# Downsampled and local attention with mixture of experts: value products in 64-row pieces, P^T in one copy, full transposes of q and k, values loaded 256 keys at a time

## The chip, the cores and the metric

The kernel runs on one core of a Trainium2 chip. The metric is the device time of one execution in microseconds (us), and lower is better. The engines are TensorE (PE, with its weight loads PEld), VectorE (DVE), ScalarE (ACT), GpSimd (POOL) and SyncE (SP, which here only issues transfers). SBUF is the working memory of 128 partitions, PSUM the memory of eight banks that PE writes.

## What is computed

There are 8 batches of 8 heads, 576 positions and 64 numbers per head. Two attentions are added, and the sum goes through eight experts, each of which takes a fixed number of tokens:

```
q_d, k_d, v_d = means of q, k, v over 4 neighbouring positions
out_up    = repeat(softmax(q_d k_d^T / 8) v_d, 4)
out_local = softmax(where(|i-j| < 4, q k^T / 8, -1e9)) v
x = (out_up + out_local) as 4608 rows of 512
logits = x w_gate;  tokens are assigned greedily, 576 to each expert
out[tokens of e] = relu(x w1[e]) w2[e]
```

## The kernel before

The program has two stages. The class `Attention` makes x and the gate's logits, and then `Routing` and `Experts` pick the tokens of one expert after another and run its two products. The change touches the attention stage alone.

**Local attention** goes by tiles: a tile u is four windows of 32 queries, so there are 36 tiles and 4.5 tiles to a batch. A window sees 38 keys. One tile passes through these steps, each of them a piece of work for PE:

- `loc_s` (line 430): 32 products of 64 rows by 32 columns, scores of 32 queries against 38 keys, into a PSUM tile "s" of two banks. DVE takes the maxima and subtracts (lines 439 and 440), and ACT exponentiates (line 442) into `sw`.
- `loc_t` (line 450): four transposes of 128x128 into a tile "g" of one bank. ACT copies it out in two copies of 64 partitions (line 461), into `ptw`, in which the blocks of two windows stand beside zeros, so that one product of 128 rows can serve two windows.
- `loc_v` (line 472): 16 products of 128 rows by 64 columns with the values `vw`, in two halves of one "g" bank each. `norm` (lines 397, 398 and 400) divides each half on DVE.
- `log_a`, `store`, `log_t` and `log_m`: DVE adds the upsampled part `up` (line 480), SP stores x, PE transposes x (line 490) and forms the logits.

**Per batch**, `trw` (line 292) turns q and k so that the 64 numbers of a head lie on partitions: eight times per batch, each time eight products of a 64-column piece with the identity, into one "g" bank that one copy of 128 partitions empties (`evac`, line 278 on ACT or line 276 on DVE). `trt` does the same for the last 64 positions. `gsum` sums groups of four on POOL and DVE, and `down_s`, `down_t` and `down_v` are the downsampled attention.

**The order** is written by hand. `run` gives each piece a due time in tiles (`LOC` for the tile's steps, `TW` and `TWS` for the transposes, `DW` for the downsampled part, `NEXT` for the loads of the next batch), sorts all pieces by it and emits them. Every engine then works through its own list in that order, and so does SP with its transfers. "g" has six buffers (`NG`) and "s" one, which is all eight banks. A transfer on SP also waits for the transfer eight places ahead of it.

**Values for the local part** are loaded by tile: `load_vw` (line 228) issues four transfers per tile, each 48 keys of one window for all eight heads, into one of four buffers. `EV` says which of the copies in `evac` go to DVE (1) and which to ACT (0), once the first 24 are past.

## Time and profile before

| what | value |
|---|---|
| median of 3 runs | 780.48 us (778.41 to 783.68) |
| profiled execution | 776.94 us, span 775.3 us (1.6 us lie around it) |
| PE busy over the span | 710.1 us (92%) |
| DVE, ACT, POOL busy | 526.9, 306.2, 222.4 us |
| attention stage | until about 288 us |

The span is the time from the first to the last instruction of the profile. "Busy" counts the time in which at least one instruction of the engine runs. Matmuls overlap in the array, so the time that a group of them costs is better read from the start of the group to the start of the next one. In a timeline row stand the start, the length, the engine, the line, what is written from what, and the count. fp32 products appear twice in the count, as two passes.

### The profile page before, as it was taken

How to read it: one execution, taken by the hardware profiler on the slowest of the kernel's cores; microseconds unless marked ns; L12 is line 12 of the kernel's file. 1: busy time of each engine (PE TensorE's matmuls, PEld its weight loads, DVE VectorE, ACT ScalarE, POOL GpSimd, SP SyncE). 2: the span in 40 equal slices, each digit the busy share in tenths (PEclk: the TensorE clock that was granted, in tenths of full speed). 3: DMA queues.
4: the chain of work that ended last, by engine and by line, in shares of the span. 5: the costliest groups of instructions: out<-in, count | busy, mean ns of one | idle time of the engine just before them, and what ended most of it. 6: DMA issues, size and time to landing. Idle time of an engine off the chain costs nothing.

```text
span 775.3 us, 22696 instructions
## 1 busy us (share of the span) xinstructions
PE 710.1 (92%) x9393; PEld 493.1 (64%) x9393; DVE 526.9 (68%) x1634; ACT 306.2 (39%) x601; POOL 222.4 (29%) x257
## 2 busy tenths in 40 slices
PE   7998999899999863699899999999989999999994
PEld 5887888787878752465465466465456475574752
DVE  3876785858667887886969989798859545271210
ACT  2444645456464440341624435144225144252210
POOL 6345262424426340300710503130320402201011
PEclk9999999999999995699999999999999999999998
DMA  9969979898998650611615554572833764704000
GB/s 262 220 191 245 241 209 262 227 242 246 235 234 200 163 176 3 209 70 62 244 36 208 144 171 157 106 268 56 258 117 110 156 245 95 199 1 102 21 28 34
DMA packets 148138, 125.09 MB, mean 161 GB/s; under 512 B 92228, under 2 KB 122436, under 8 KB 148036
## 3 DMA queue, kind: packets, MB, share of 16 engines
q1 hardware_dynamic: 140656, 102.12, 48.6%
q0 software_dynamic: 6432, 20.98, 8.9%
q8 instruction: 74, 1.21, 0.7%
q10 hardware_dynamic: 948, 0.55, 0.3%
q14 instruction: 28, 0.23, 0.1%
HBM read 95.30 MB, written 21.23 MB: 150 GB/s over the span
## 4 chain that ended last, share of the span: by engine, by line
PE 44%; issue 25%; DVE 18%; POOL 4%; DMA 4%; ACT 2%; another core or an unknown queue 1%; SPq 0%; POOLq 0%; ACTq 0%; DVEq 0%
PE g L292 8%; PE pH L1109 8%; PE pX L1148 6%; PE g L472 3%; POOL out_dram L1157 2%; DVE cmp L698 2%; PE g L318 2%; PE s L430 2%; DVE wl L1055 2%; PE g L366 2%; PE g L450 2%; PE pR L728 2%; PE g L490 1%; PE g L363 1%; DVE ht L1135 1%
## 5 line engine op out<-in xcount | busy, mean ns | idle before, releaser
L1109 PE MATMUL pH<-xt,wh 128*128 128x256 f16 (+1 forms) x1024 | 200.0, 289 | 1.7 <-ACT xt L1084 0.7
L1148 PE MATMUL pX<-wh,ht 128*128 128x512 f16 (+1 forms) x640 | 180.6, 380 | 1.9 <-DVE xt L1085 1.9
L1109 PE MATMUL pH<-xt,wl 128*128 128x320 f16 (+1 forms) x512 | 147.7, 289 | 0.0
L1148 PEld LDWEIGHTS <-ht 128*128 128x128 f16 (+1 forms) x960 | 81.6, 100 | 90.4 <-issue 5.9
L1157 POOL DMA_INDIRECT out_dram<-y,idx x40 | 44.9, 1123 | 282.5 <-ACT y L1154 260.2
L1148 PE MATMUL pX<-wl,ht 128*128 128x512 f16 (+1 forms) x320 | 117.9, 380 | 0.0
L1109 PEld LDWEIGHTS <-wh 128*128 128x128 f16 x1024 | 97.9, 98 | 28.3 <-issue 3.4
L1132 ACT ACTIVATE ht<-pH 128x512 f16<-128x512 f32 (+1 forms) x128 | 45.5, 408 | 126.4 <-PE pH L1109 123.9
L1055 DVE SCALAR_TENSOR_TENSOR wl<-nat,wh 128x512 f16<-128x512 f32 x128 | 84.8, 684 | 2.2
L1070 POOL DMA_INDIRECT xg<-x_dram,idx x40 | 49.2, 1231 | 103.9 <-DVE idx L999 34.5
L1135 DVE SCALAR_TENSOR_TENSOR ht<-pH,ht 128x512 f16<-128x512 f32 (+1 forms) x128 | 52.6, 451 | 33.8 <-ACT ht L1132 33.3
L1154 ACT ACTIVATE y<-pX 128x512 f32<-128x512 f32 (+1 forms) x40 | 23.7, 594 | 129.7 <-PE pX L1148 76.4
L292 PE MATMUL g<-ident,nat 128*64 128x128 f32 x1024 | 69.8, 282 | 0.7 <-issue 0.3
L1053 ACT ACTIVATE wh<-nat 128x1024 f16<-128x1024 f32 x64 | 66.6, 1056 | 9.3 <-DMA nat<-in_moe_w_dram 9.2
L292 PEld LDWEIGHTS g<-ident,nat 128*64 128x64 f32 x1024 | 56.4, 139 | 8.0 <-issue 3.7
L1109 PEld LDWEIGHTS <-wl 128*128 128x128 f16 x512 | 50.4, 98 | 12.4 <-issue 0.4
L461 ACT COPY pt<-g 64x512 f32<-64x512 f32 x72 | 41.7, 579 | 25.3 <-PE g L450 24.5
L1156 DVE SCALAR_TENSOR_TENSOR y<-pX,y 64x512 f32<-64x512 f32 x8 | 5.5, 693 | 59.1 <-ACT y L1154 59.0
L472 PE MATMUL g<-vw,pt 128*64 128x65 f32 x1152 | 43.4, 226 | 1.9 <-DMA x_dram<-x 0.9
L472 PEld LDWEIGHTS g<-vw,pt 128*64 128x64 f32 x1152 | 38.1, 139 | 7.7 <-ACT pt L461 3.9
L278 ACT COPY qt<-g 128x512 f32<-128x512 f32 (+1 forms) x32 | 19.0, 593 | 43.6 <-PE g L292 37.0
L728 PEld LDWEIGHTS <-cmp 128*128 128x128 bf16 x504 | 20.2, 97 | 24.2 <-DVE cmp L698 12.3
(218 smaller groups left out, 1137.2 us busy)
## 6 DMA issues: line engine op xcount, KB each, us to landing
nat<-in_moe_w_dram SPq DMA_DIRECT2D x28, 1024.0 KB
vw<-in_v_dram SPq DMA_DIRECT2D x136, 96.0 KB
up<-up_dram SPq DMA_DIRECT2D x36, 256.0 KB
x_dram<-x SPq DMA_DIRECT2D x36, 256.0 KB
nat<-in_q_dram SPq DMA_DIRECT2D x16, 512.0 KB
nat<-in_k_dram SPq DMA_DIRECT2D x16, 512.0 KB
nat<-in_v_dram SPq DMA_DIRECT2D x14, 512.0 KB
up_dram<-xu SPq DMA_DIRECT2D x16, 128.0 KB
```

What stands on the lines that cost most here:

```text
L292: nc.tensor.matmul(p[64 * s:64 * s + 64, :, f], src[:, 2 * hp + s, f], self.ident, start=True, stop=True)
L461: self.nc.scalar.copy(out, in_)
L472: nc.tensor.matmul(o[64 * i:64 * i + 64, 65 * h:65 * h + 65], pt[:, 2 * (h % 2) + i, 2 * g + h // 2].rearrange("p b q -> p (b q)"), self.v ...
L728: mm = nc.tensor.matmul(cv[:m * J, :, :m], cmp[:, t:t + m].rearrange("p t j -> p (t j)"), oh[:, :, t:t + m], start=t == 0, stop=t + m == N ...
L1053: nc.scalar.activation(hi, r, AF.Copy, scale=sc)
L1055: nc.vector.scalar_tensor_tensor(lo[:, a:a + LOP], r[:, a:a + LOP], sc, hi[:, a:a + LOP], op0=OP.mult, op1=OP.subtract)
L1070: self.fetched = nc.gpsimd.indirect_dma_start(out=xg[:n], out_offset=None, in_=self.x, in_offset=bass.IndirectOffsetOnAxis(ap=idx[:n, c:c ...
L1109: mm = nc.tensor.matmul(p[:, s, :s1 - s0], w[d][a][:, 128 * f:128 * f + 128], xt[:, b, d, s0:s1], start=j == 0, stop=j == len(seq) - 1)
L1132: last = nc.scalar.activation(hi, q, AF.Relu)
L1135: nc.vector.scalar_tensor_tensor(lo, q, 0.0, hi, op0=OP.max, op1=OP.subtract)
L1148: mm = nc.tensor.matmul(p[o:o + m], ht[:, f, h0:h0 + m], w[4 + f // 2][b][:, 512 * (f % 2):512 * (f % 2) + 512], start=j < parts, stop=j > ...
L1157: i = nc.gpsimd.indirect_dma_start(out=self.out, in_=y[:n], in_offset=None, out_offset=bass.IndirectOffsetOnAxis(ap=idx[:n, c:c + 1], axis=0))
```

## The change

It does five things.

1. `trw` uses full transposes of 128x128: two of the four positions of a group and their 64 numbers at once. There are four of them per call, for two pairs of heads and one half of each pair. The result stands on two halves of the partitions, so two copies of 64 partitions empty the bank, both on the same engine.
2. `loc_t` empties its bank in one copy of 128 partitions by 512 (`ptw` loses its zeros), and `sw` is ordered by window first.
3. `loc_v` makes a product for each window and head, 64 rows by 32 columns, at positions in the array that depend on the head's half and the window. It writes to a tile "s" of two banks, and one division serves the whole tile of 128x512.
4. The pool "g" has four buffers and "s" two.
5. Values are loaded by head in groups of eight windows (`load_vw`), eight transfers per group and two groups per batch; the first and last window of a batch are loaded apart (`load_ve`). There are three buffers of a group. Of `evac`'s calls one in four goes to DVE.

```diff
-NG = 6
+NG = 4
+NS = 2
-EV = (0,)
+EV = (0,0,0,1)
+VG = 8
+VS = 0.06
...
+    def load_ve(self, b, w):
...
+            for i in range(2):
+                p0 = 64 * i + r0
+                nc.sync.dma_start(self.ve[b % 2][p0:p0 + n, int(w > 0), :, :D],
...
+    def load_vw(self, b, w, m, h):
+        n, i = divmod(w - 1, VG)
+        t = self.vw[(2 * b + n) % 3]
+        p0 = 64 * (h % 2)
+        self.nc.sync.dma_start(t[p0:p0 + VR, i:i + m, h // 2, :D],
...
-        for f in range(4):
-            for s in range(2):
-                nc.tensor.matmul(p[64 * s:64 * s + 64, :, f], src[:, 2 * hp + s, f], self.ident, start=True, stop=True)
-        self.evac(self.dest(b, which)[:, hp, :4 * GM], p.rearrange("p g f -> p (g f)"))
+        for a in range(2):
+            for fp in range(2):
+                nc.tensor.transpose(p[:, a, :, fp], src[:, 4 * hh + 2 * a + s, 2 * fp:2 * fp + 2].rearrange("p f d -> p (f d)"),
+                                    self.ident)
+        t = self.dest(b, which)[64 * s:64 * s + 64, 2 * hh:2 * hh + 2]
+        for par in range(2):
+            self.evac(t[:, :, par:4 * GM:2], p[64 * par:64 * par + 64].rearrange("p a i f -> p a (i f)"), par)
...
-            self.pevac(a, out[r, :, :, a], p[r].rearrange("p (i h q) -> p i h q", h=4, q=QW))
+        nc.scalar.copy(self.ptw[u % NPT].rearrange("p c h q -> p (c h q)"), p)
...
-        for h in range(4):
-            for i in range(2):
-                nc.tensor.matmul(o[64 * i:64 * i + 64, 65 * h:65 * h + 65],
-                                 pt[:, 2 * (h % 2) + i, 2 * g + h // 2].rearrange("p b q -> p (b q)"),
-                                 self.vw[u % 4][:, i, 4 * g + h], start=True, stop=True)
-        self.norm(o, x[:, 256 * g:256 * g + 256].rearrange("p (h d) -> p h d", h=4), 4, 1.0)
+        for hp in range(HP):
+            for c, vw in cs:
+                for i in range(2):
+                    r = slice(64 * i, 64 * i + 64)
+                    nc.tensor.matmul(o[32 * c:32 * c + 32, i, hp], pt[r, c, hp], vw[r, hp], start=True, stop=True,
+                                     tile_position=(64 * i, 32 * c))
+        if g == 0:
+            return
...
+        nc.vector.tensor_scalar(r, o[..., D], 1e-9, None, op0=OP.add)
+        nc.vector.reciprocal(r, r)
+        nc.vector.tensor_tensor(x.rearrange("p (h i d) -> p i h d", i=2, d=D), o[..., :D],
+                                r[..., None].to_broadcast([128, 2, HP, D]), op=OP.mult)
```

The order of the pieces stays the same; what stands in them changes. On PE, behind the third batch's `trt`, before (natt, sd and nat are the sources of the transposes, vw and pt those of the value products):

```order
L302 MATMUL g<-ident,natt 64x128 x8
L348 MATMUL g<-ident,sd 128x128 x3
L472 MATMUL g<-vw_128,pt_132 64x65 x16
L348 MATMUL g<-ident,sd 128x128 x3
L292 MATMUL g<-ident,nat 64x128 x8
L348 MATMUL g<-ident,sd 128x128 x3
L353 MATMUL g<-ident,sdt 128x128 x2
L292 MATMUL g<-ident,nat 64x128 x8
L450 MATMUL g<-ident,sw_129 128x128 x4
```

And now:

```order
L316 MATMUL g<-ident,natt 64x128 x8
L362 MATMUL g<-ident,sd 128x128 x3
L479 MATMUL s<-vw_126,pt_133 32x65 x32
L362 MATMUL g<-ident,sd 128x128 x3
L303 MATMUL g<-ident,nat 128x128 x4
L362 MATMUL g<-ident,sd 128x128 x3
L367 MATMUL g<-ident,sdt 128x128 x2
L303 MATMUL g<-ident,nat 128x128 x4
L464 MATMUL g<-ident,sw_130 128x128 x4
```

No row moved. Eight products of 64 columns became four of 128, and sixteen value products became thirty-two, which write to "s" instead of "g".

On ACT, in the same batch, the copies out of the banks before (qt and kt are the turned q and k, ptd and pt the transposed probabilities):

```order
L278 COPY ptd<-g 128x384
L278 COPY qt<-g 128x512
L278 COPY ptd<-g 128x384
L278 COPY ptd<-g 128x256
L278 COPY kt<-g 128x512
L461 COPY pt_132<-g 64x16x32 x2
L278 COPY qt<-g 128x512
L442 ACTIVATE sw_129<-sw_129 128x8x38
```

And now:

```order
L289 COPY ptd<-g 128x384
L289 COPY qt<-g 64x2x256 x2
L289 COPY ptd<-g 128x384
L289 COPY kt<-g 64x2x256 x2
L466 COPY pt_133<-g 128x512
L289 COPY qt<-g 64x2x256 x2
L456 ACTIVATE sw_130<-sw_130 128x8x38
```

Each copy of q or k became two, the two copies of pt became one, and one of the ptd copies went to DVE.

On SP, around the end of a batch's downsampled part (up_dram and up carry it through memory), before:

```order
L380 DMA up_dram<-xu 128x256
L387 DMA up_dram<-xu 8x16x64
L409 DMA up<-up_dram 128x1x512
L228 DMA vw_126<-in_v_dram 48x8x64 x3
L228 DMA vw_126<-in_v_dram 32x8x64
L228 DMA vw_126<-in_v_dram 6x8x64
L214 DMA nat<-in_q_dram 128x4x256
L483 DMA x_dram<-x 128x512
L214 DMA nat<-in_k_dram 128x4x256
L409 DMA up<-up_dram 128x1x512
L214 DMA nat<-in_v_dram 128x4x256
L228 DMA vw_127<-in_v_dram 48x8x64 x4
```

And now:

```order
L394 DMA up_dram<-xu 128x256
L401 DMA up_dram<-xu 8x16x64
L423 DMA up<-up_dram 128x1x512
L232 DMA ve_129<-in_v_dram 32x4x64 x2
L232 DMA ve_129<-in_v_dram 6x4x64 x2
L215 DMA nat<-in_q_dram 128x4x256
L497 DMA x_dram<-x 128x512
L215 DMA nat<-in_k_dram 128x4x256
L423 DMA up<-up_dram 128x1x512
L215 DMA nat<-in_v_dram 128x4x256
L232 DMA ve_128<-in_v_dram 48x4x64 x2
L240 DMA vw_127<-in_v_dram 48x8x64 x5
```

The other transfers stand where they stood. The value loads come in runs of eight now, and a batch has 22 of them where it had 19.

More of the change, by code (lines that the diff above doesn't have):

```diff
@@ L126, in __init__ @@
             self.vd.append(cst.tile([128, 2, H, D + 1], F32, name=f"vd{i}"))
-        for i in range(4):
-            self.vw.append(cst.tile([128, 2, H, D + 1], F32, name=f"vw{i}"))
+        for i in range(3):
+            self.vw.append(cst.tile([128, VG, HP, D + 1], F32, name=f"vw{i}"))
+        for i in range(2):
+            self.ve.append(cst.tile([128, 2, HP, D + 1], F32, name=f"ve{i}"))
         for i in range(NSW):
@@ L131, in __init__ @@
         for i in range(NPT):
-            self.ptw.append(cst.tile([128, 4, 4, 2, QW], F32, name=f"pt{i}"))
+            self.ptw.append(cst.tile([128, 4, HP, QW], F32, name=f"pt{i}"))
     def gate(self):
@@ L148, in fixed @@
         if part == 0:
-            for t in self.vw[:2]:
+            for t in (self.ve[0], self.vw[0]):
                 nc.gpsimd.memset(t, 1.0)
@@ L418, in loc_s @@
         if g == 0:
-            self.so[u] = self.ps.tile([128, 2, 512], F32, name="s", bufs=1)
+            self.so[u] = self.ps.tile([128, 2, 512], F32, name="s", bufs=NS)
             for i in range(2):
@@ L451, in loc_t @@
                                 self.ident)
-        out = self.ptw[u % NPT]
-        for a in range(2):
-            r = slice(64 * a, 64 * a + 64)
-            self.pevac(a, out[r, :, :, a], p[r].rearrange("p (i h q) -> p i h q", h=4, q=QW))
-    def pevac(self, a, out, in_):
-        if PEV[a]:
-            self.nc.vector.tensor_copy(out, in_)
-        else:
-            self.nc.scalar.copy(out, in_)
+        nc.scalar.copy(self.ptw[u % NPT].rearrange("p c h q -> p (c h q)"), p)
     def loc_v(self, u, g):
@@ L514, in transposes, with f @@
         out = []
-        for hp in range(HP):
-            for w in "qk":
-                def f(w=w, hp=hp):
-                    self.trw(b, w, hp)
-                    if b and hp % 2 and w == "k":
-                        self.gsum(b, "k", hp - 1)
-                        self.gsum(b, "q", hp - 1)
-                        if hp == 3:
-                            self.gsum_v(b)
-                out.append(f)
+        for hh in range(2):
+            for s in range(2):
+                for w in "qk":
+                    def f(w=w, hh=hh, s=s):
+                        self.trw(b, w, hh, s)
+                        if b and s and w == "k":
+                            self.gsum(b, "k", 2 * hh)
+                            self.gsum(b, "q", 2 * hh)
+                            if hh:
+                                self.gsum_v(b)
+                    out.append(f)
         return out[:2] + [lambda: self.trt(b)] + out[2:]
@@ L597, in run @@
                     work += [(at + SPACE * k, 3, k, lambda g=steps: next(g, None), False) for k in range(24)]
+        for b in range(B):
+            for w in (0, NW - 1):
+                if b or w:
+                    work.append(((b * NW + w) // 4 - VWT, 0, 0, lambda b=b, w=w: self.load_ve(b, w), False))
+            for n in range(2):
+                z = b * NW + 1 + VG * n
+                at = z // 4 - VWT
+                old = z - (NW + 1 if n else 2 * NW + 1 - 2 * VG)
+                if old > 0:
+                    at = max(at, old // 4 + LOC["v1"] + 0.0005)
+                for w, m, at in ((1, 3, LD0[2] + 0.01), (4, 5, LD0[3])) if at < -1.0 else ((1 + VG * n, VG, at),):
+                    for h in range(H):
+                        work.append((at + VS * h, 0, h, lambda b=b, w=w, m=m, h=h: self.load_vw(b, w, m, h), False))
         work.sort(key=lambda z: z[:3])
```

52 lines of the change are left out of this document (26 added, 26 removed).

## The prediction

> **What bounds the kernel now.** The change lies in the attention stage, so I first read busy time by stretch. The columns are the stretch, its length, then the busy time of PE, PEld, DVE, ACT and POOL, the granted clock of PE, the busy share of the DMA engines and their GB/s.
>
> ```profile
> 20.00:260.00 240.00, 229.38 (x5186) 193.68 (x5185) 174.71 (x483) 127.19 (x268) 103.08 (x138) 0.99 0.91 229
> ```
>
> PE is busy in 229.4 of 240 us; 10.6 us are idle. No other engine comes near: DVE 73%, ACT 53%. The transfers are at 0.91. The chain of waits through the same stretch says which work sets the pace:
>
> ```profile
> by line: PE g L292 22.5%; PE g L472 10.2%; PE g L318 6.6%; PE s L430 5.5%; PE g L450 5.4%; PE g L366 4.9%; PE g L490 4.1%; PE g L348 4.0%; PE g L363 3.6%; issue 2.8%; PE g L302 2.6%; DVE gtmp L265 2.5%; ACT pt L461 1.9%; DVE x L480 1.9%; PE
> ```
>
> The transposes of q and k (L292) are 22.5% of it and the value products (L472) 10.2%, and both are rewritten. So PE sets the pace, and what the change does to PE's work is nearly the whole gain or loss, until the next resource is reached. That one is SP with its transfers:
>
> ```profile
> 129.39 2.22 SPq L228 DMA_DIRECT2D vw<-in_v_dram  x4
> 132.19 0.35 SPq L483 DMA_DIRECT2D x_dram<-x  x1
> 132.60 0.54 SPq L409 DMA_DIRECT2D up<-up_dram  x1
> 133.23 3.00 SPq L228 DMA_DIRECT2D vw<-in_v_dram  x4
> 136.28 0.46 SPq L214 DMA_DIRECT2D nat<-in_q_dram  x1
> 136.79 0.51 SPq L214 DMA_DIRECT2D nat<-in_k_dram  x1
> 137.39 0.45 SPq L380 DMA_DIRECT2D up_dram<-xu  x1
> 137.89 0.68 SPq L483 DMA_DIRECT2D x_dram<-x  x1
> ```
>
> From 129.39 to 137.89 SP issues for 7.53 of 8.50 us, 89%. Over 240 us that is an estimate of 213 us, some of it time in which the rings were full. The rings themselves are uneven:
>
> ```profile
> 120.00:140.00 20.00, 19.95 (x437) 16.97 (x433) 11.44 (x34) 11.26 (x25) 6.78 (x9) 1.00 1.12 278
> 200.00:220.00 20.00, 18.81 (x494) 16.00 (x490) 15.72 (x50) 9.31 (x17) 11.23 (x16) 1.00 0.78 191
> ```
>
> They move 278 GB/s in one stretch of 20 us and 191 in another, so 229 on the average is not their limit. The 55.0 MB of the 240 us (229 x 240) would take 198 us at 278.
>
> **The change, part by part.** The prices on PE are read from starts in PE's timeline, from one group to the next:
>
> ```profile
> 120.59 1.15 PE L472 MATMUL g<-vw,pt 128*64 128x65 f32 x32
> 121.67 0.55 PE L348 MATMUL g<-ident,sd 128*128 128x128 f32 x3
> 122.15 1.09 PE L292 MATMUL g<-ident,nat 128*64 128x128 f32 x16
> 123.18 0.26 PE L505 MATMUL g<-wg,xt 128*128 128x16 f16 x4
> ...
> 125.09 0.66 PE L450 MATMUL g<-ident,sw 128*128 128x128 f32 x4
> 125.58 0.29 PE L421 MATMUL s<-mask,identb 128*128 128x152 bf16 x2
> 125.81 0.77 PE L430 MATMUL s<-kt,qt 64*32 64x38 f32 x64
> 126.51 1.10 PE L292 MATMUL g<-ident,nat 128*64 128x128 f32 x16
> ...
> 128.92 0.61 PE L490 MATMUL g<-ident,x 128*128 128x128 f32 x4
> 129.45 1.09 PE L292 MATMUL g<-ident,nat 128*64 128x128 f32 x16
> ...
> 131.95 0.66 PE L375 MATMUL g<-vd,ptd 128*32 128x65 f32 x32
> 132.54 1.15 PE L472 MATMUL g<-vw,pt 128*64 128x65 f32 x32
> ```
>
> *Transposes on PE.* A call of `trw` costs 1.03 us (122.15 to 123.18). Four full transposes are what `loc_t` and `log_t` already issue: 0.49 us (125.09 to 125.58) and 0.53 (128.92 to 129.45). I take 0.51, so a call saves 0.52. There are 64 calls, 56 of them for the batches after the first: 56 x 0.52 = 29.1 us in the stretch above. The bounds are 28.0 and 30.2.
>
> *Value products on PE.* Sixteen products of 128x64 cost 1.08 us per tile (120.59 to 121.67). Thirty-two of 64x32 with 65 columns do not occur; the nearest rows are L430, 64 passes of 64x32 with 38 columns in 0.70 us, and L375, 32 passes of 128x32 with 65 columns in 0.59, which is 1.18 for 64. L430 is the nearer in tiling and L375 in columns. I take no change, between the two. The bounds for 36 tiles are 36 x (0.70 - 1.08) = -13.7 and 36 x (1.18 - 1.08) = +3.6 us. If the two halves of 64 rows did not work beside each other, only two column groups would be busy, as in L472: 64 x 1.08/32 = 2.16 per tile, +39 us. The 0.70 us of L430, which uses both halves, speaks against it.
>
> *The copies.* A copy goes by its length, not by its partitions:
>
> ```profile
> L461 ACT COPY pt<-g 64x512 f32<-64x512 f32 x72 | 41.7, 579 | 25.3 <-PE g L450 24.5
> L278 ACT COPY qt<-g 128x512 f32<-128x512 f32 (+1 forms) x32 | 19.0, 593 | 43.6 <-PE g L292 37.0
> L276 DVE COPY qt<-g 128x512 f32<-128x512 f32 (+1 forms) x8 | 5.5, 683 | 10.1 <-PE g L292 8.4 <-PE g L302 1.1 <-PE s L430 0.6
> L397 DVE TENSOR_SCALAR den<-g 128x4 f32<-128x4 f32 (+1 forms) x83 | 12.8, 154 | 22.2 <-PE g L472 18.5 <-PE g L366 3.5
> L398 DVE RECIPROCAL den<-den 128x4 f32<-128x4 f32 (+1 forms) x83 | 14.9, 179 | 2.9
> L400 DVE TENSOR_TENSOR x<-g,den 128x256 f32<-128x256 f32 x67 | 28.4, 424 | 2.3
> ```
>
> On ACT the copies of q and k go from 56 to 90 (34 x 0.58 = +19.7 us), those of P^T from 72 halves to 36 whole (36 x 0.593 - 72 x 0.579 = -20.3), and eight of ptd go to DVE (about -4). ACT is no fuller than before. On DVE, 30 more copies of q and k at 0.68 are +20.5 us and ptd +4.4. The division drops from two of 0.154 + 0.179 + 0.424 to one of 0.154 + 0.179 + about 0.68 (a read of 512 from PSUM, as in L276): 36 x 0.50 = -18. So DVE gets about 7 us more and stands at 181 us. That fits beside PE's 200, and I cost it at nothing; if PE's cover goes it is a bound at 181. The single P^T copy lets `loc_v` start 0.57 us sooner; PE waited little for it (L461 is 1.9% of the chain), and I take 0, with -4 us as its bound.
>
> *Banks.* "g" loses two of six banks but also the two tiles per u of `loc_v`. A `trw` bank is now held for 0.51 + 2 x 0.58 = 1.7 us and more where ACT is late. I take 0; if every second copy showed on PE, 56 x 0.58 = +32 us.
>
> *Loads.* The bytes are the same, but there are 184 transfers where there were 152:
>
> ```profile
> L228 SPq DMA_DIRECT2D vw<-in_v_dram x152: 311/470/1920, 9.2 to 269.3; - x152
> ```
>
> At the median of 0.47 us, 32 more cost SP 15 us, about 12 of them in the stretch. They are issued ahead of `nat`, `up` and x, which wait behind them in SP's list.
>
> *The first batch.* Its eight calls run in a row:
>
> ```profile
> 6.85 7.25 PE L292 MATMUL g<-ident,nat 128*64 128x128 f32 x128
> ```
>
> They would need 8 x 0.51 = 4.1 us on PE, but sixteen copies shared by ACT and DVE take 8 x 0.63 = 5.0, so about 2 us are saved (0 to 3).
>
> *The sum.* PE's work in the stretch falls to 229.4 - 29.1 = 200.3; with the idle time of today, 10.6, it would take 211 us. SP's estimate of 213 rises to 225. The higher of the two decides: 240 - 225 = 15 us, and 2 at the start, **-17 us**. Of PE's 29 us, 14 are lost to SP and the transfers. The tail after 260 us and the experts do not change. The profiled execution took 776.94 us, 1.6 around its span; less 17 that is 760. The median of the three runs stands 3.5 above the profiled one, so the forecast for the median is 763.5, and I give **764 us**.
>
> **The rivals.**
>
> *All of PE's saving arrives.* If SP's 213 us are to a good part full rings that later work can fill, PE stays the pace: -29 - 2 = -31, 749 us. For it speaks the stretch at 191 GB/s, which has room; against it that the loads come in runs of eight.
>
> *The second copy stands in the place of the saved PE time.* Four banks, each held by two copies on one engine: +32 against -31, about 781 us, no change. For it speaks that PE's next transposes need a bank of that pool; against it that the pool now serves fewer tiles and that ACT is only half busy.
>
> *The clock.* PE falls to half its clock at times. The first row, of PE's timeline, shows it standing still for 1.75 us, and the second, of the stretches, the clock just behind (0.50):
>
> ```profile
> 142.52 0.26 PE L430 MATMUL s<-kt,qt 64*32 64x38 f32 x3 [1.75 <-issue]
> ```
>
> ```profile
> 143.60:146.80 3.20, 3.20 (x70) 2.78 (x73) 3.10 (x8) 1.36 (x3) 2.96 (x4) 0.50 0.12 35
> ```
>
> A PE with more gaps may fall more often. One such stretch of 3.2 us costs 1.6; with one in each half batch, 14 x 1.6 = 22 us go and about -9 is left on the full saving, 772 us. [...]
>
> *SP becomes the pace and pays its waits on top: slower.* SP works in order, and it waits for things that no faster PE brings sooner:
>
> ```profile
> SPq L409 <- DMA up_dram<-xu: 13.7, 7, 2.8
> SPq L228 <- PE g L292: 5.0, 7, 1.4
> SPq L387 <- DMA nat<-in_k_dram: 4.4, 5, 1.1
> ```
>
> Here 11% of 240, 27 us, are waits. If all stay, 213 + 12 + 27 = 252 us, +12, and with the start +10: about 790 us. It decides from the point at which more than 15 us of the 27 stay. For it speak the 13.7 us behind up_dram; against it that the waits on PE (L228) shrink, and that the values of a group have a buffer that was free for a tile longer.
>
> **How the numbers follow.** A measurement tells about 1% (8 us) from no change. Chances: forecast 0.45, all of the saving 0.18, second copy 0.14, clock 0.06, SP slower 0.17. The forecast's own range is 756 to 773. Faster by over 1% are the second case, nearly all of the first and a third of the clock's: 0.64. Within 1% lie the copies and the rest of the clock and of the first: 0.20. Slower by over 1%: SP's case, less its mild end, 0.16. The range reaches to the full saving and a part of SP's case: 750 to 786.
>
> **What would show it.** In the profile after, right: a group of four transposes every 0.5 us with 32 products of 64x32 at about 1.1 us per tile; PE busy near 200 us in what was 20 to 260; the stage shorter by 13 to 20 us; a higher mean GB/s; more of PE's idle time behind transfers or copies. Wrong: PE waiting for ACT or DVE ahead of the transposes (banks), value products near 2 us per tile, half-clock stretches in every batch, or a stage that ends later with SP issuing throughout. The experts should take the same time.

## The result, and the profile after

The changed kernel takes 791.47 us (median of 14 runs, 784.27 to 794.52) beside 780.75 us for the kernel before (14 runs, 775.97 to 783.72). The ratio is 1.0132, 95% interval 1.0105 to 1.0158: **1.3% slower**, where 2% faster was forecast. The profiled execution took 788.88 us, with a span of 787.2 us, 11.9 us longer than before. All of that lies in the attention stage: its last logits product starts at 287.7 us before and at 299.7 us after.

PE did lose its work. The same stretch of the stage, in the same columns as in the prediction (length, busy PE, PEld, DVE, ACT, POOL, granted clock, share of the DMA engines, GB/s), of the changed kernel:

```profile
20.00:260.00 240.00, 198.09 (x5131) 168.05 (x5135) 175.53 (x402) 119.87 (x246) 95.92 (x132) 0.90 0.89 221
```

PE is busy for 198.1 us, and 200.3 was forecast. But the idle time, 10.6 us before, is now 41.9 (240 - 198.1), and the granted clock is 0.90 on the average where it was 0.99. (The two stretches hold nearly the same work, the later one some 10 us less of it.) Over the whole stage, from 18 us to the start of the last logits product, PE's busy time fell from 252.3 to 231.9 us and its idle time rose from 17.5 to 49.8: 20.4 us won, 32.3 lost, 11.9 net. So the agreement of 198.1 with 200.3 is in part luck: over the stage PE lost 20.4 us of busy time, not the 29.1 that the prediction took off, and the later stretch holds less work.

PE's own lines fill less of the chain of waits through the stretch:

```profile
by line: PE s L479 9.1%; issue 8.9%; PE s L444 6.7%; DMA up<-up_dram 6.7%; PE g L303 6.3%; PE g L464 5.7%; PE g L504 5.5%; PE g L332 4.9%; DMA nat<-in_q_dram 3.9%; DMA nat<-in_v_dram 3.3%; SPq L240 3.3%; ACT qt L289 2.6%; DMA nat<-in_k_dram
```

The transposes of q and k (L303, before L292 with 22.5%) are 6.3%. In their place stand "issue" at 8.9% (before 2.8%), transfers of `up`, q, v and k, and SP's own issuing. The groups of PE up to the end of the attention stage show the same. Behind the bar are busy time and the mean in ns of one pass, then the idle time just before the group and what ended it. First the kernel before, then the changed one:

```profile
L292 PE MATMUL g<-ident,nat 128*64 128x128 f32 x1024 | 69.8, 282 | 0.7 <-issue 0.3 <-DVE lg L510 0.2
L472 PE MATMUL g<-vw,pt 128*64 128x65 f32 x1152 | 43.4, 226 | 1.9 <-DMA x_dram<-x 0.9 <-issue 0.5 <-ACT pt L461 0.4
```

```profile
L479 PE MATMUL s<-vw,pt 64*32 64x65 f32 x2048 | 44.3, 245 | 12.4 <-issue 12.1 <-ACT pt L466 0.3
L303 PE MATMUL g<-ident,nat 128*128 128x128 f32 x256 | 41.9, 292 | 13.8 <-DMA nat<-in_q_dram 6.2 <-DMA nat<-in_k_dram 3.7 <-ACT qt L289 1.7
L504 PE MATMUL g<-ident,x 128*128 128x128 f32 x144 | 26.8, 313 | 4.4 <-issue 4.4
L464 PE MATMUL g<-ident,sw 128*128 128x128 f32 x144 | 26.0, 310 | 11.2 <-ACT sw L456 5.5 <-ACT qt L289 2.7 <-issue 1.6
L479 PE MATMUL s<-ve,pt 64*32 64x65 f32 x256 | 10.7, 237 | 0.0
```

The transposes lost 27.9 us of busy time (69.8 to 41.9) and gained 13.1 us of waits for transfers and copies ahead of them. The value products gained 11.6 us of busy time (44.3 + 10.7 - 43.4) and 10.5 us of waits, nearly all of them "issue": PE stood still, and no semaphore that the profile shows held it. Part of the added busy time goes with the lower clock: a tile's products take 1.04 us in a stretch at 1.00 and 1.50 us in one at 0.50 (rows below).

**The prices were right.** Starts in PE's timeline of the changed kernel:

```profile
127.78 1.01 PE L479 MATMUL s<-vw,pt 64*32 64x65 f32 x64
128.82 0.55 PE L362 MATMUL g<-ident,sd 128*128 128x128 f32 x3
129.21 0.60 PE L303 MATMUL g<-ident,nat 128*128 128x128 f32 x4
129.64 0.25 PE L519 MATMUL g<-wg,xt 128*128 128x16 f16 x4
```

```profile
153.59 1.57 PE L479 MATMUL s<-vw,pt 64*32 64x65 f32 x64
155.09 0.27 PE L519 MATMUL g<-wg,xt 128*128 128x16 f16 x4
```

A call of `trw` takes 0.43 us (129.21 to 129.64; 0.51 was taken; 0.46 is the median of 48 calls at full clock) and a tile's value products 1.04 us (127.78 to 128.82; 1.08 was taken) where nothing disturbs them. The second pair of rows shows the products at a granted clock of 0.50: 1.50 us. The two halves of 64 rows do work beside each other, by the 1.04 us; one after the other would have been near 2.2 us, by the prediction's estimate.

**Where PE stands still.** One of the longest gaps of the stage:

```profile
148.53 0.44 PE L504 MATMUL g<-ident,x 128*128 128x128 f32 x2
153.07 0.59 PE L504 MATMUL g<-ident,x 128*128 128x128 f32 x2 [4.11 <-issue]
```

In the middle of one block of four transposes PE stops for 4.11 us. Between 150.5 and 152.5 us the instruction queue carried one packet (the columns are packets, MB and the share of 16 engines), and the clock fell just behind:

```profile
q8 instruction: 1, 0.02, 3.1%
```

```profile
145.80:149.20 3.40, 2.75 (x127) 2.34 (x128) 2.89 (x8) 0.88 (x2) 3.19 (x6) 1.00 1.00 308
149.20:152.60 3.40, 0.00 (x0) 0.00 (x0) 1.54 (x2) 0.46 (x1) 3.17 (x4) 1.00 0.67 224
152.60:156.00 3.40, 2.92 (x78) 2.42 (x78) 1.33 (x4) 0.60 (x1) 1.87 (x4) 0.50 0.23 76
156.00:159.40 3.40, 3.40 (x120) 2.69 (x121) 2.21 (x6) 1.37 (x3) 0.00 (x0) 0.50 0.42 52
```

The packet (16 KB, on the queue from 150.9 to 151.8 us) lies inside the gap, and the gap ends 1.2 us behind it. Each of the long issue gaps looks like that: at 225.0 us (4.46 us long, packet from 222.6) and at 283.3 us (3.22 us, packet from 281.1). The traces of the two kernels have nine issue gaps of PE over 0.9 us in the attention stage (seven here, two in the kernel before), and each ends 1.2 to 1.8 us behind the landing of a packet on this queue. The number of packets falls with PE's instructions as well: up to 300 us there are 50 here and 37 in e1 below, which has 3,456 matmuls and weight loads fewer. From this I take it that PE waited for its own instructions; the profile names no releaser. The waits with "issue" as releaser come to 23.3 us in the stage, beside 4.4 before.

**Where the loads stand.** SP at the start, first before, then after. The rows of `nat` with q and k are those of the second batch, and the last row of each is the third batch's q:

```profile
8.66 0.38 SPq L214 DMA_DIRECT2D nat<-in_v_dram  x1
9.16 2.86 SPq L228 DMA_DIRECT2D vw<-in_v_dram  x4
...
13.28 0.63 SPq L214 DMA_DIRECT2D nat<-in_q_dram  x1
13.95 0.82 SPq L214 DMA_DIRECT2D nat<-in_k_dram  x1
...
38.06 0.47 SPq L214 DMA_DIRECT2D nat<-in_q_dram  x1
```

```profile
8.58 0.38 SPq L215 DMA_DIRECT2D nat<-in_v_dram  x1
9.07 1.00 SPq L232 DMA_DIRECT2D ve<-in_v_dram  x2
10.40 0.31 SPq L240 DMA_DIRECT2D vw<-in_v_dram  x1
...
11.52 6.06 SPq L240 DMA_DIRECT2D vw<-in_v_dram  x7
17.62 0.44 SPq L215 DMA_DIRECT2D nat<-in_q_dram  x1
18.10 0.51 SPq L215 DMA_DIRECT2D nat<-in_k_dram  x1
...
44.92 0.47 SPq L215 DMA_DIRECT2D nat<-in_q_dram  x1
```

Where four transfers of values stood ahead of q and k, ten stand now. The second batch's q goes out at 17.62 instead of 13.28 us, the third's at 44.92 instead of 38.06. SP as a whole is no fuller: up to 300 us it spends 219.8 us on issuing 368 transfers, before 218.3 on 336.

### The profile page after: what moved, and what is told of

It is laid out like the page before. It is cut to its first block, busy times and chain, and to the rows that moved or that the text cites. A ratio compares the mean times of both kernels' runs of the same rounds, so it can differ in the third digit from the quotient of the medians.

```text
span 787.2 us, 23431 instructions
## 1 busy us (share of the span) xinstructions
PE 688.6 (87%) x9777; PEld 474.6 (60%) x9777; DVE 542.0 (69%) x1566; ACT 303.5 (39%) x589; POOL 217.2 (28%) x256
## 4 chain that ended last, share of the span: by engine, by line
PE 41%; issue 23%; DVE 18%; DMA 9%; ACT 3%; POOL 3%; SPq 2%; POOLq 0%; ACTq 0%; DVEq 0%
PE pH L1135 10%; PE pX L1174 7%; PE s L479 4%; PE s L444 3%; PE g L464 2%; PE g L504 2%; POOL out_dram L1183 2%; PE pR L754 2%; DVE cmp L724 2%; DMA up<-up_dram 2%; PE g L303 2%; PE g L332 2%; DMA nat<-in_v_dram 2%; DVE wl L1081 2%; DVE ht L1161 1%
## 5 line engine op out<-in xcount | busy, mean ns | idle before, releaser
L1135 PEld LDWEIGHTS <-wh 128*128 128x128 f16 x1024 | 97.5, 98 | 28.7 <-issue 4.2
L1096 POOL DMA_INDIRECT xg<-x_dram,idx x40 | 44.3, 1107 | 104.8 <-DVE idx L1025 34.7
L479 PE MATMUL s<-vw,pt 64*32 64x65 f32 x2048 | 44.3, 245 | 12.4 <-issue 12.1
L303 PE MATMUL g<-ident,nat 128*128 128x128 f32 x256 | 41.9, 292 | 13.8 <-DMA nat<-in_q_dram 6.2
L479 PEld LDWEIGHTS s<-vw,pt 64*32 64x32 f32 x2048 | 36.2, 119 | 20.2 <-issue 19.1
L289 ACT COPY kt<-g 64x512 f32<-64x512 f32 (+1 forms) x56 | 35.2, 629 | 22.8 <-PE g L303 22.4
L289 ACT COPY qt<-g 64x512 f32<-64x512 f32 (+1 forms) x46 | 28.5, 619 | 35.2 <-PE g L303 29.0
L303 PEld LDWEIGHTS g<-ident,nat 128*128 128x128 f32 x256 | 30.2, 148 | 18.9 <-issue 7.8
L466 ACT COPY pt<-g 128x512 f32<-128x512 f32 x36 | 21.1, 585 | 40.5 <-PE g L464 40.2
```

The costliest lines, as they stand in the source:

```text
L289: self.nc.scalar.copy(out, in_)
L303: nc.tensor.transpose(p[:, a, :, fp], src[:, 4 * hh + 2 * a + s, 2 * fp:2 * fp + 2].rearrange("p f d -> p (f d)"), self.ident)
L479: nc.tensor.matmul(o[32 * c:32 * c + 32, i, hp], pt[r, c, hp], vw[r, hp], start=True, stop=True, tile_position=(64 * i, 32 * c))
L1096: self.fetched = nc.gpsimd.indirect_dma_start(out=xg[:n], out_offset=None, in_=self.x, in_offset=bass.IndirectOffsetOnAxis(ap=idx[:n, c:c ...
L1135: mm = nc.tensor.matmul(p[:, s, :s1 - s0], w[d][a][:, 128 * f:128 * f + 128], xt[:, b, d, s0:s1], start=j == 0, stop=j == len(seq) - 1)
```

## The experiments

Each ratio is to the kernel before, run on the same chip, with its 95% interval. The chips differ: on them the kernel before took 773 to 781 us, so a time that was expected in us is best compared through the ratio. "Points" are hundredths of the kernel's time before.

The expectations name their theories by letters. F: PE waits for its own instructions. S: SP's list and the value loads set the pace. B: two copies hold each bank. K: what PE saves becomes waits and half clock. L: the loads by group (with the banks), or their place ahead of q and k, cost the time. D: behind SP stands the chain of DVE, exponentials and transposes.

The profiled stages of the main runs, summed from each trace (from 18 us to the start of the last logits product, in us; "half clock" is time at a granted clock of 0.50):

| kernel | ratio | stage ends | PE busy | PE idle | half clock | idle: ACT / issue / DMA / DVE |
|---|---|---|---|---|---|---|
| before | 1 | 287.7 | 252.3 | 17.5 | 7.7 | 8.2 / 4.4 / 0.9 / 0.7 |
| after | 1.0132 | 299.7 | 231.9 | 49.8 | 59.5 | 15.3 / 23.3 / 8.3 / 1.5 |
| e1, wide products | 1.0036 | 295.8 | 224.0 | 53.8 | 69.6 | 24.1 / 3.8 / 10.5 / 9.2 |
| e4, transposes alone | 0.9968 | 291.6 | 231.5 | 42.1 | 44.9 | 25.1 / 5.6 / 4.1 / 4.4 |
| e5, the same, PE kept busy | 1.0014 | 292.1 | 242.4 | 31.7 | 21.1 | 21.9 / 4.4 / 3.1 / 1.5 |
| e6, the same as e4, few loads | 0.9773 | 275.4 | 226.7 | 30.7 | 38.3 | 22.8 / 1.1 / 2.9 / 1.5 |
| e14, wide, no transposes | 1.0111 | 294.2 | 246.3 | 30.0 | 23.6 | 12.2 / 7.2 / 1.1 / 5.3 |

One profiled execution is not the median: of e4 the stage ended later than before, while its median is lower. The times decide, the table tells what kind of waiting there was. Waits that POOL ended are not in it, and "ACT" holds the exponentials as well as ACT's copies.

### Is PE the bound at all? (e2)

In the kernel before each value product is split in two, of 33 and 32 columns.

```diff
+                for d0, d1 in ((0, 33), (33, 65)):
+                    nc.tensor.matmul(o[64 * i:64 * i + 64, 65 * h + d0:65 * h + d1],
...
+                                     self.vw[u % 4][:, i, 4 * g + h, d0:d1], start=True, stop=True)
```

> The kernel before, in which each value product is done as two, of 33 and of 32 columns: PE has as many instructions in the value products as the changed kernel, everything else stays, and the result is complete. Theory F: PE's waits without a releaser grow by 5 to 20 us and the half clock comes with them, 788 to 805. Theories S and B: only what PE itself takes longer, at most 0.2 us for a tile, 780 to 788.

Measured: 819.61 beside 780.92 us, 1.0466 (1.0353 to 1.0579), more than either expected. PE's busy time in the stage grew by 36.1 us (252.3 to 288.4) and the stage by 39.9. The issue waits grew with the passes, from 4.4 to 14.0 us, within the 5 to 20 us more that F expected, while other waits shrank. The group, of which the trace holds most records:

```profile
L473 PE MATMUL g<-vw,pt 128*64 128x33 f32 (+1 forms) x1986 | 67.6, 226 | 4.1 <-issue 3.6 <-ACT pt L461 0.4
```

A pass with 33 columns lasts as long as one with 65 (226 ns in both). And added PE work comes out in the time nearly one to one. The first claim of the prediction holds in this direction: PE set the pace of the kernel before.

### The transposes alone (e4, e13, e5)

e4 is the kernel before with part 1 of the change (`trw`, `transposes`, EV (0,0,0,1)), "g" still with six banks. e13 is e4 with all copies on ACT once the first 24 are past. e5 is e4 with six products of 512 columns that nothing reads, ahead of `loc_t` in the last tiles of each batch.

```diff
...
-                nc.tensor.matmul(p[64 * s:64 * s + 64, :, f], src[:, 2 * hp + s, f], self.ident, start=True, stop=True)
-        self.evac(self.dest(b, which)[:, hp, :4 * GM], p.rearrange("p g f -> p (g f)"))
...
+                nc.tensor.transpose(p[:, a, :, fp], src[:, 4 * hh + 2 * a + s, 2 * fp:2 * fp + 2].rearrange("p f d -> p (f d)"),
+                                    self.ident)
+        t = self.dest(b, which)[64 * s:64 * s + 64, 2 * hh:2 * hh + 2]
+        for par in range(2):
+            self.evac(t[:, :, par:4 * GM:2], p[64 * par:64 * par + 64].rearrange("p a i f -> p a (i f)"), par)
```

```diff
+        for _ in range(6 if 2 * u % 9 >= 5 else 0):
+            nc.tensor.matmul(p, self.wm, self.wm[:, None].to_broadcast([128, 4, 128]), start=True, stop=True)
```

> The kernel before with the change's first part alone: full transposes of q and k, two copies each, one of four copies on DVE; six banks, the old value products and loads. Theory F: PE has 33 us less work and fewer instructions, so most of it arrives: 752 to 764, with no more half-clock stretches than before. Theory B: the second copies take it back: 775 to 785. [...] Theory S: 752 to 766, since no transfer is added.

> The transposes alone with every copy on ACT (EV all 0); complete. DVE is at 85% of the stage once the loads are gone, and it runs late where the adds wait for the upsampled part. If DVE's share of the copies holds PE up: 3 to 8 us less than the transposes alone. If ACT's two copies in a row do: 2 to 10 us more.

> The transposes alone (the run e4_transposes) with six bf16 products of 512 columns, whose results are overwritten, ahead of the transposes of P^T in the last two tiles of each batch, where PE waits for the exponentials: 16 tiles, about 1.3 us each at full clock. The result is complete. Theory K (PE's saved time becomes waits, any 3.4 us in which PE is busy for less than some 0.6 of the time are followed by half clock, and that costs the saving): the 45 us at half clock fall below 25, and the time falls by 3 to 10 us, 769 to 776. If the half clock costs nothing, because what PE waits for comes no sooner: 778 to 790.

e4: 779.08 beside 780.92 us, 0.9968 (0.9935 to 1.0000). The part that was to bring the whole gain brings 0.3%, and 0.65% at most. The stretch and the transposes of P in e4:

```profile
20.00:260.00 240.00, 205.92 (x4374) 177.78 (x4375) 190.36 (x511) 142.32 (x282) 104.34 (x139) 0.92 0.89 226
```

```profile
L453 PE MATMUL g<-ident,sw 128*128 128x128 f32 x144 | 24.3, 294 | 14.9 <-ACT sw L445 9.1 <-ACT qt L278 3.4 <-POOL gtv L240 1.6
```

PE's work is gone and its idle time has grown by more than that: 17.5 to 42.1 us in the stage. ACT ended 25.1 us of it: 9.1 with the exponentials (L445) that `loc_t` needs, 7.9 with copies of q and k (1.5 before), most of the rest with its other copies. e13: 771.81 beside 773.46 us, 0.9979 (0.9955 to 1.0003). With every copy on ACT the waits that copies of q and k end are longer, 11.1 us, those that the exponentials end shorter, 3.3 us, and the time is the same. So how the copies are shared isn't what holds it, and neither are the four banks of "g", which e4 doesn't have. That there are two copies to a call is a part of the new waits; a kernel with one copy was not run. e5: 775.48 beside 774.97 us, 1.0014 (0.9985 to 1.0043). The fillers halved the half-clock time (44.9 to 21.1 us) and PE's idle time fell by 10.4 us, its busy time rose by 10.9, and nothing was won (775.48 us lies in the first theory's range only because this chip runs the kernel before in 774.97 us). What the lost clock costs is left open by that: the fillers' own time may have used up what the clock gave back.

### What hides the transposes' gain? (e6, e7; e10, e17, e15)

e6 is e4, and e7 the kernel before, with the values of the local part loaded for the first four tiles only.

```diff
     def load_vw(self, u):
...
+        if u > 3:
+            return
```

> The transposes alone, in which only the first four tiles' values are loaded: it leaves out the value loads of the other 32 tiles, 12.5 MB, and reuses what stands in the buffers. Theory S (SP with its transfers is what PE's saving runs into): most of the 33 us now arrive, 745 to 757. Theory K: 765 to 778, since the chain of PE, DVE and ACT has the same waits.

> The kernel before with the same value loads left out, as the counterpart. Theory S: PE is the pace here, so little falls, 773 to 780, and the run with the new transposes is 20 us or more faster. Theory K: within 6 us of the run with the new transposes.

e7: 769.76 beside 774.97 us, 0.9943 (0.991 to 0.9976). e6: 756.31 us, 0.9773 (0.9703 to 0.9843). With these loads the transposes bring 0.3 points (0 to 0.65); without them 1.7 (0.9943 to 0.9773, known to some 0.8), about 13 us. So **the value loads hide most of what the transposes can bring**, four fifths by the medians. The rest of the 33 us (64 calls at 0.52) that were taken from PE doesn't come even then, and neither theory had it right: S expected 20 us or more between e6 and e7, K at most 6. Whether the loads hide it by their place in SP's list or by the room that their bytes take in the DMA engines was not told apart: leaving them out empties both (the DMA engines' share falls from 0.89 in e4 to 0.61). Stretch, and SP's waits, of e6 (engine and line, what it waited for, us, times, longest):

```profile
20.00:260.00 240.00, 213.84 (x4734) 186.38 (x4734) 204.77 (x550) 149.87 (x300) 108.00 (x145) 0.92 0.61 185
```

```profile
SPq L384 <- DVE xu L404: 35.4, 8, 8.2
SPq L487 <- DVE x L484: 26.5, 11, 4.8
```

SP now waits for results, and DVE is at 85%. ACT ended 22.8 us of PE's idle time. What sets the pace there, DVE's load or the length of the chain from the scores over the exponentials to the next transposes, wasn't told apart.

e10 is e4 with the x stores issued by POOL and not by SP; e17 is the kernel before with the same; e15 moves the reads of `up` to POOL as well.

```diff
-UPQ = STQ = "sync"
+UPQ = "sync"
+STQ = "gpsimd"
```

> The transposes alone, with the 36 stores of x issued by GpSimd instead of SP; complete. If it is SP's list in order (its issue time of about 0.43 us for each store and its waits for x) that the saving runs into: 5 to 12 us less than the transposes alone, 766 to 773 where the kernel before has 780. If it is the bytes in the rings: within 3 us of the transposes alone.

> The kernel before with the x stores issued by POOL and not by SP, nothing else. If SP's list holds the work back only when PE has less to do: 0.998 to 1.003. If the stores on SP cost the kernel before as much as they cost with part 1 (0.5%): 0.993 to 0.997.

> The kernel before with part 1 alone (e4), and x stores and `up` reads issued by POOL and not by SP. S (SP's list holds back the saving): below 0.990, at least as fast as with the x stores alone (0.9916). D (behind SP stands the chain DVE, exp, transpose): no more than with the x stores alone, 0.990 to 0.994; POOL's own work delaying `up` would give over 0.995.

e10: 768.51 beside 773.46 us, 0.9916 (0.9883 to 0.9949). e17: 769.81 beside 774.57 us, 0.9945 (0.9917 to 0.9973). e15: 773.12 us, 1.0001 (0.9977 to 1.0025). Thirty-six entries fewer in SP's list are worth 0.5 points with the transposes and 0.55 without. (Whether it is the place in SP's list or the room in SP's queue that the stores leave free was not told apart.) So the stores cost time, but it isn't they that hide the transposes: between e17 and e10 these bring 0.3 points, as from the kernel before to e4. The expectation that SP's list binds only when PE has less to do was wrong. e15 was a miss: moving `up` to POOL loses it all again, and in its profile PE waits 8.4 us for POOL. **e10 is complete and 0.84% faster than the kernel before**, the fastest complete version of this study.

### The value products (e1, e14, e12)

e1 is the changed kernel with the products of four head pairs in one of 260 columns, 8 to a tile instead of 32. The other three pairs take the P^T of the first, so three quarters of it are left out.

```diff
-        for hp in range(HP):
-            for c, vw in cs:
...
+        for c, vw in cs:
+            for i in range(2):
+                r = slice(64 * i, 64 * i + 64)
+                nc.tensor.matmul(self.o[u][32 * c:32 * c + 32, i, :HP * (D + 1)], pt[r, c, 0],
+                                 vw[r].rearrange("p h d -> p (h d)"), start=True, stop=True,
...
```

> The changed kernel, in which each of the value products of a window and half takes all four head pairs at once: 8 products of 64x32 with 260 columns for a tile instead of 32 with 65. The array streams the same columns, the waits and loads stay, and PE has 96 instructions less per tile. It leaves out three quarters of P^T: all four pairs take the first pair's probabilities. Theory F (PE waits for its own instructions, which arrive in blocks of 16 KB: 23 us of PE's idle time in the stage has no releaser but 'issue', and each such gap ends some 1.4 us behind the landing of an instruction block): the gaps fall back to about the 4 us of the kernel before and the half-clock stretches behind them go too, so 20 to 30 us less than the changed kernel, 760 to 772. Theory S (SP's queue and the value loads set the pace): within 4 us of the changed kernel, 787 to 795. Theory B (two copies hold each of four banks): unchanged too.

> The change without its first part: the old products of 64 columns with one copy, all copies on ACT, and the rest as changed; complete. Theory F with theory K: PE is the pace again, so its waits without a releaser (20 us in the changed kernel) come on top, 790 to 805. If the transposes with their two copies are what costs in the changed kernel: 775 to 785.

> The changed kernel without part 1 (the old `trw`), EV (0,), and the value products of a tile in 8 wide products of 64x32 with 260 columns instead of 32 with 65; all columns of four head pairs take the P^T of the first pair, so three quarters of P^T are left out. Parts 2 to 5 alone cost +2.05% (e12). F (PE waits for its own instructions, which the small products make more of): without the small products most of the 2% goes, 0.998 to 1.010. L (loads by group and the banks): the cost is not in the products, 1.015 to 1.025.

e1: 783.74 beside 780.92 us, 1.0036 (1.0001 to 1.0071), 1.0 points below the changed kernel. The group in e1:

```profile
L478 PE MATMUL s<-vw,pt 64*32 64x260 f32 x512 | 28.7, 428 | 0.3 <-DVE lg L524 0.3
```

The issue waits ahead of the products are gone (12.1 us to none) and those of the stage fell from 23.3 to 3.8; the products' busy time fell too, 55.0 to 28.7 us. The instruction queue carried 37 packets up to 300 us instead of 50, for 3,456 matmuls and weight loads fewer. Only 8 us of all this came out in the time. In the table the waits for ACT, DMA and DVE took the freed place (together 25.1 before the edit, 43.8 with it). e12, the changed kernel with the transposes of before and EV (0,): 792.33 beside 773.46 us, 1.0205 (1.0158 to 1.0251). So parts 2 to 5 alone cost 2.0%, and on top of them the transposes bring 0.7 points. e14, e12 with wide products: 781.27 beside 774.57 us, 1.0111 (1.0074 to 1.0147), just above the range in which most of the 2% would have gone. The small products are again worth some 0.9 points, about half of what parts 2 to 5 cost.

Since the wide products have fewer instructions and less work at once, e1 and e14 price the small products as they are. They don't show how much of it is the wait for instructions.

### The loads by group (e3, e9, e11)

e3 is the changed kernel, e9 is e1, each with only the first three groups of values loaded (104 transfers left out). e11 spreads the eight transfers of a group over more time.

```diff
     def load_vw(self, b, w, m, h):
         n, i = divmod(w - 1, VG)
+        if 2 * b + n > 2:
+            return
```

```diff
-VS = 0.06
+VS = 0.2
```

> The changed kernel, in which only the first three groups of values are loaded: it leaves out the other value loads of whole groups, 104 transfers of 96 KB, and reuses what stands in the buffers. Theory S: the stage is freed, 30 us or more less, 755 to 765. Theory F: the waits without a releaser stay for the most part, since PE has the same instructions, and only the waits on transfers (8 us) and what the instruction blocks gain from emptier rings go: 772 to 785. Theory B: 785 to 792.

> The changed kernel with the wide value products of e1_wide_v and the few loads of e3_few_loads together; it leaves out what both leave out. If instruction blocks and transfers each hid the other (both had to go): 745 to 757. If a third thing holds the stage (theory K): 762 to 772.

> The changed kernel with the eight loads of a group spread over 1.6 tiles instead of 0.5 (VS 0.2); complete. If the runs of eight hold up the loads of q, k and the upsampled part behind them: 4 to 8 us less than the changed kernel. If only the sum of the transfers counts: within 3 us of it.

e3: 772.33 beside 780.92 us, 0.9893 (0.9805 to 0.998), 2.4 points below the changed kernel; a like cut in the kernel before gave 0.6 (e7). The issue waits stay in e3, as F expected: 20.1 us in its stage, with the DMA engines at 0.66 of the stretch in place of 0.89. So it isn't the value loads that make PE wait for its instructions. e9: 755.37 beside 774.97 us, 0.9767 (0.9695 to 0.984), the same as e6 with 0.9773, each known to 0.7 points. So without the loads, and with wide products, all of the rest of the change (one copy of P^T, four banks) costs nothing that shows; with the loads e1 stands 0.7 points above e4. That this 0.7 is the cost of the loads by group is argued from the two pairs and not shown: it is no larger than what the pair without loads leaves open, the two cuts aren't alike (e9 still loads the first and last window of each batch), and the wide products are lighter than those of before. e11: 786.23 beside 773.46 us, 1.0144 (1.0103 to 1.0186): the runs of eight do no harm that shows by being runs.

### Their place in SP's list (e16, e18, e19)

e16 is the changed kernel with the x stores issued by POOL. e18 is the changed kernel with the values a tile later, so that q and k go out ahead of them. e19 does both.

```diff
-VWT = 1.75
+VWT = 0.75
...
-                for w, m, at in ((1, 3, LD0[2] + 0.01), (4, 5, LD0[3])) if at < -1.0 else ((1 + VG * n, VG, at),):
+                for w, m, at in ((1, 3, -0.28), (4, 5, 0.25)) if b == n == 0 else ((1 + VG * n, VG, at),):
```

> The changed kernel with the x stores issued by POOL and not by SP. S: SP's list matters there as much as with part 1 alone (0.5%), 1.004 to 1.010 against 1.0132. F: PE's own instructions and the start set the pace, 1.010 to 1.016.

> The changed kernel, with the values loaded one tile later (VWT 0.75, at the start the first two groups at -0.28 and 0.25 tiles), so that the second batch's q and k go out ahead of them on SP and the later q and k before each group. L (the values stand ahead of q and k in SP's list and push the start back): 1.003 to 1.008 against 1.0132. F (the order of the loads doesn't matter, only the number of instructions and transfers): 1.011 to 1.016. If the values then come too late for their products: over 1.016.

> The same, and the x stores issued by POOL and not by SP, which took 1.1% off the changed kernel and 0.55% off the one before. If the two savings are of the same list and don't add: 1.000 to 1.004. If they add: 0.992 to 0.998, beside 0.9916 for part 1 alone with the x stores on POOL.

e16: 775.21 beside 774.57 us, 1.0018 (0.9986 to 1.005), 1.1 points below the changed kernel and better than either theory had it. The 36 stores cost the kernel before 0.55 points and the changed one twice that, a difference just beyond the noise (0.6, known to 0.5): an entry in SP's list seems to weigh more there. The issue waits stay, 21.0 us. e18: 786.22 beside 780.26 us, 1.0085 (1.0052 to 1.0117). In its SP list the second batch's q now stands ahead of the values that come by group:

```profile
11.19 0.41 SPq L215 DMA_DIRECT2D nat<-in_q_dram  x1
11.65 0.51 SPq L215 DMA_DIRECT2D nat<-in_k_dram  x1
...
17.59 7.53 SPq L240 DMA_DIRECT2D vw<-in_v_dram  x8
...
36.06 0.79 SPq L215 DMA_DIRECT2D nat<-in_q_dram  x1
```

The third batch's q goes out at 36.06 us, 8.9 us sooner than after, and the time falls by 0.5 points, just outside of what L expected, and the intervals of the two overlap a little. e19: 784.74 us, 1.0041 (1.0009 to 1.0072). The two savings don't add: 1.1 and 0.5 points apart, 0.9 together. That fits with time in the same list, and just as well with e18's 0.5 points being partly noise.

## Why the prediction was wrong

The range (750 to 786) missed the time and the sign was wrong; a slower kernel had been given a chance of 0.16. By its own steps:

1. *PE bounds the stage.* Right for added work (e2: 36 us more, 40 us longer) and misleading for removed work (e4: 20.8 us less busy in the stage, 2.5 us shorter).
2. *Transposes on PE, 29.1 us in the stretch.* The price was right, even a little high: 0.43 us a call in place of 0.51. In all 27.9 us of busy time went, of the 33 that all 64 calls stand for. It wasn't the gain.
3. *Value products, no change.* Right as a price, 1.04 us per tile in place of 1.08, at full clock. Missing in the sum was what so many small instructions do to PE itself: 23.3 us of issue waits beside 4.4. The step priced a block by its length and its neighbours' and gave the stream of instructions no cost. With wide products, which are also less work, 1.0 points came back.
4. *Copies.* DVE was forecast at 181 us and has 175.5 in the stretch. e13 shows that it doesn't matter whose the copies are. The rows answering to those of before: ACT's copies of q and k last a little longer than the 0.58 taken, the single copy of P^T and the one division are as forecast.

```profile
L289 ACT COPY kt<-g 64x512 f32<-64x512 f32 (+1 forms) x56 | 35.2, 629 | 22.8 <-PE g L303 22.4
L466 ACT COPY pt<-g 128x512 f32<-128x512 f32 x36 | 21.1, 585 | 40.5 <-PE g L464 40.2
L488 DVE TENSOR_TENSOR x<-s,dl 128x512 f32<-128x512 f32 x36 | 24.9, 691 | 1.2
```

5. *Banks, 0.* No run speaks against it: e9 with four banks stands where e6 with six does. The rival of the second copy (no change, 781) has about the right time for e4, but e4 has six banks, and its 32 us are too many: copies of q and k ended 7.9 us of PE's waits in e4 and 6.9 in the changed kernel, beside 1.5 before. They are a part of what took the saving's place.
6. *Loads, 12 us more on SP, and the higher of PE and SP decides.* **This is the step that failed.** It took PE's work with today's 10.6 us of idle time (211), added 12 us to SP's 213, and let the higher of the two be the time. e4 tests that rule by itself, since it adds no transfer: the rule gives 240 - 213 and 2 at the start, 29 us, and 2.5 came. The idle time that the rule held fixed grew instead: with the transposes alone from 17.5 to 42.1 us in the stage, ended by exponentials, copies and transfers. Some 11 of the 13 us that the transposes can bring are hidden by the value loads (e6 and e7, by the medians); the rest of their 33 us doesn't come without the loads either, and PE waits for exponentials and copies there. SP's term was wrong too. The 8.5 us that were read are fuller than the rest: the profile before has SP issuing for 191.7 of the 240 us, and its total did not grow with the change (219.8 us up to 300 us, 218.3 before). No run shows how much of the issue time, if any, was spent on full rings. With the right total the rule would have let all of PE's saving arrive, 749 us, and been further off. What the loads by group cost isn't in the total. What was seen beside it is the order in the list, with q, k and `up` behind longer runs of values, about 0.5 points and hardly clear of noise (e18), and the 36 stores, 1.1 points in place of 0.55 (e16). The prediction named that ("`nat`, `up` and x, which wait behind them") and gave it no price.
7. *First batch, -2.* Confirmed, -1.6: 5.62 us of transposes and waits for transfers (6.29 to 11.91) stand in the place of 7.25.

```profile
6.29 1.92 PE L303 MATMUL g<-ident,nat 128*128 128x128 f32 x16
8.90 0.63 PE L303 MATMUL g<-ident,nat 128*128 128x128 f32 x4 [0.69 <-DMA nat<-in_q_dram]
10.48 1.50 PE L303 MATMUL g<-ident,nat 128*128 128x128 f32 x12 [0.95 <-DMA nat<-in_k_dram]
11.91 1.09 PE L316 MATMUL g<-ident,natt 128*64 128x128 f32 x16
```

Put together from the runs: transposes alone -0.3 points (e4), from there to e1 +0.7 (loads by group, banks, one copy of P^T and wide products), from e1 to the changed kernel +1.0 (small products). The three come to the 1.3 measured by the way they are taken, so the sum proves nothing; each difference is known to some 0.5 points. The rival in which SP becomes the pace gave 790 us and the time was 791. That is luck in good part: the rival had the place right for what the loads cost, but SP's total didn't grow, and by the medians the largest part of the loss, the small products, was elsewhere. The clock's rival was about right in amount, 14 stretches of 3.2 us, 45 us in all: there are eleven half-clock stretches of 59.5 us, beside three of 7.7 before. Its time, 772, was not, and whether these stretches cost anything beyond the gaps ahead of them stays open (e5). They aren't the small products' doing, since e1 has 69.6 us of them.

Open are also the split of the small products' cost between waiting for instructions and the work itself, whether the value loads act through SP's list or through the DMA engines, and what holds the stage of e6 once the loads are gone.

## What to carry to other kernels

That an engine is busy 95% of a stage tells what added work costs, not what removed work brings: take the next resource out in a trial (here the value loads) before counting the saving. In a list that is worked through in order, price a new transfer by what is queued behind it, not only by its share of the list's total. And count instructions, not only their busy time, where many small ones stand in for a few large ones.

## What was new of the hardware

- **The granted clock fell behind gaps of PE, and not behind a window of transposes.** In the traces of the kernels before and after, each stretch at a granted clock of 0.50 that begins in the attention stage or reaches into it lasts 3.41 us or a multiple of it (3.41 to 13.65 us after). I cut both stages (from 18 us on) into windows of that length, in step with the clock's changes. Twelve windows at a granted clock of 1.00 (ten after, two before) were followed by one at 0.50, and PE was busy for 0.00 to 0.63 of each. In the 129 that were followed by one at 1.00 PE was busy for 0.60 or more of each. The first two rows are two windows of the changed kernel, then two where the clock falls; the second block is what PE did in the first of them:

```profile
128.70:132.10 3.40, 2.87 (x34) 2.49 (x29) 2.00 (x6) 2.99 (x9) 0.00 (x0) 1.00 1.30 212
132.10:135.50 3.40, 3.33 (x86) 2.85 (x84) 0.95 (x2) 3.24 (x7) 2.13 (x3) 1.00 1.09 312
74.10:77.50 3.40, 1.22 (x68) 1.06 (x57) 3.30 (x7) 0.93 (x2) 2.35 (x3) 1.00 1.10 321
77.50:80.90 3.40, 3.40 (x128) 2.73 (x127) 3.30 (x7) 1.43 (x3) 3.11 (x6) 0.50 1.04 352
```

```profile
L303 PE MATMUL g<-ident,nat 128*128 128x128 f32 x8 | 1.3, 279 | 0.5 <-ACT qt L289 0.5
L362 PE MATMUL g<-ident,sd 128*128 128x128 f32 x6 | 1.1, 291 | 0.0
L464 PE MATMUL g<-ident,sw 128*128 128x128 f32 x4 | 0.6, 272 | 0.0
```

From 128.7 us PE is busy for 0.84 of the window (2.87 of 3.40), but only for 0.12 with anything other than transposes, and the clock stays at 1.00 in the next one. From 74.1 us it is busy for 0.36, and the clock falls to 0.50. So in this window the fp32 transposes went with full clock as PE's other work did.

- **A value product's pass of 33 columns took as long as one of 65.** Halving the columns of the value products from 65 to 33 left a pass at 226 ns (e2), so that twice the passes took some 36 us more: 31 ns for each of the 1,152 more, with its weight load, beside 34 ns (1.08 us for 32) for a pass of 65.
- **PE stood still until a packet of instructions had landed**, for up to 4.46 us at a time in the changed kernel (the gap that ends at 225.0 us), where the 32 small products of a tile go by in about 1 us (1.04), 64 passes and their weight loads. All nine such gaps over 0.9 us, in the traces before and after, end 1.2 to 1.8 us behind the landing of a 16 KB packet on the instruction queue. Leaving the value loads out (e3) leaves 20.1 of the 23.3 us of issue waits, and with fewer and wider products they fall to 3.8 us (e1).
